# Reordering the first loads and splitting more of the first feed-forward group in a fused recurrence and ReGLU kernel

## Chip, cores and metric

The kernel runs on one core of one Trainium2 chip. The metric is device time in microseconds of one execution: the median of the runs made, and, beside it, one profiled execution whose trace gives the starts and durations of instructions. Engines: PE is TensorE (matmuls), DVE VectorE, ACT ScalarE, POOL GpSimd, SP SyncE (here it only issues DMAs).

## The reference

```python
# q, k, v, f_logit: (4 batches, 8 heads, 768 steps, 48) float32
f = 1 / (1 + exp(-f_logit))
for t in range(768):
    state = f[:, :, t, :, None] * state + k[:, :, t] (outer) v[:, :, t]
    y[:, :, t] = q[:, :, t] @ state
x = y with the heads side by side                    # (3072 tokens, 384)
out = (relu(x @ w_gate) * (x @ w_val)) @ w_out       # d_ff = 1536
```

A gated linear recurrence with a decay for each channel is followed, token by token, by a feed-forward layer with a gate.

## The kernel before

**Units.** The recurrence is cut into chunks of 128 steps. A unit `u` is two chunks of one batch (`y` = 0 and 1); `seq` gives the order of the 12 units: the first unit of each of the four batches (0 to 3), then the second ones, then the third. A unit loads f, k, v and q (`load`, L578, four DMAs of 384 KB on SP), takes exponential and logarithm of f on ACT (L669, L671), sums them along time on PE ("sums", L678, L679; for units with `even` on DVE one half is subtracted on DVE, L682), takes the exponentials of the sums and of their negatives on ACT (L690 to L700), and multiplies k and q by them on DVE or POOL ("products", `hats`, L712, L718). The products are transposed into `qkT`, on PE with a copy by DVE or ACT for the units in `pe_hats` (L770, L780), and by DMA on SP for the others. PE then forms the scores (L806), which are masked either on DVE straight from PSUM (L820) or by a copy on ACT and a product on POOL (L815, L817). Copies of v with padding (`vpad`, and `vrest` for `pe_hats` units, L753, L758) feed the state update (L860 or L871, then L638 to L646) and the output of the unit (`out_of`: 32-column form, L904, for chunks in `pe_x`, else the natural form, L911 and L915, with a DMA transpose). "Totals" (L843, L847) give the decay over a chunk; units with `td` get it through DRAM (`rates`, L827, L836) instead.

**Feed-forward groups.** Two units make a group of 512 tokens. `ffn_hidden` (L940) runs for each of 12 blocks of 128 hidden channels three matmuls for the gate (L952 with `wg`), a relu on ACT (L958), three matmuls for the value (L952 with `wv`) and a product on DVE (L964). A "triple" below is one such set of three matmuls. `ffn_out` (L969) runs the output projection with `wo` (L980, three matmuls a step) and DMAs the result. All feed-forward matmuls are in one chain, so their order is fixed. In the first group, blocks 0 to 2 are run twice on halves of 256 tokens (first unit 0's, then unit 1's), and blocks 3 to 11 on all 512.

**Weights.** Each of `w_gate`, `w_val` and `w_out` is loaded in four slices of three blocks (`wg0` to `wg3` and so on), with conversion to bf16, by DMAs that POOL issues (`load_w`, L606). The string `first` gives the order of the first loads: one order for SP's loads, one for POOL's slices. `x@y` means that the issuing engine waits for the landing of y before it issues x. A load on SP also waits for the landing of the load eight places before it (L577). Engines are in order: everything behind a waiting issue on SP or POOL waits too.

**Order.** The whole program is put in order when it is built: `Plan.schedule` runs a model of the engines, the PSUM banks and the two DMA queues (`Rings`), picks the next instruction by the time it could start and a priority, and writes out a fixed order for each engine. `Plan.limits` gives how many PSUM banks each kind may hold (`f`: feed-forward). Durations in the model (`occ`, `lat`, `RATE`) only decide the order. `EASY` and `slack` add time to modelled DMA landings after a given time. `pace` holds back the sums of a unit until a given block of the feed-forward work. Up to 24 us of modelled time, gaps of PE are filled with matmuls on zeros (L1050, "fillers").

```python
first = 'f0 k0 v0 q0 v1 f1 q3 q1 k1 wg0@k1 wv0@k0 wg1@f0 wv1@k0 wg2@f0 wv2@q0 wg3@q3 wo0@k0 wv3@f0 q2 wo2@q2 wo3@k0 wo1@f1 f2 k2 f3 k3@wg0 v2 v3'.split()
...
behind = list(after) + (sent[-8:][:1] if len(sent) >= 8 else [])
...
for r0, r1, js in {0: [(0, 2, range(0, 3)), (2, 4, range(0, 3)), (0, 4, range(3, 12))]}.get(g, [(0, GC, range(NJ))]):
    for at, j in enumerate(js):
        ffn_hidden(g, r0, r1, j)
```

Of the kernel before, what the change touches and what calls it, by code (L numbers as in the profile page):

```python
# [52 lines left out]
class Rings:  # L53


    CAP, LAND = 3300, 1.0
    RATE = {"hw": (1.0, 0.21), "sw": (1.0, 0.69)}
# [3 lines left out]
    def __init__(self):  # L61
        self.now = 0.0
        self.passed = 0
        self.coming = []
        self.queue = {r: [] for r in self.RATE}
        self.left = {r: 0.0 for r in self.RATE}
        self.out = {r: 0 for r in self.RATE}
        self.n = 0
# [9 lines left out]
    def speed(self, ring):  # L78
        return self.RATE[ring][1 if self.queue[self.OTHER[ring]] else 0]

    def worked(self, t, ring):
        work = t - self.now
        if ring == "sw":
            return work
        for p in self.PAUSES[self.passed:]:
            if p >= t:
                break
            work -= max(0.0, min(t, p + self.PAUSE) - max(self.now, p))
        return work

    def later(self, work, ring):
        t = self.now
        if ring == "sw":
            return t + work
        for p in self.PAUSES[self.passed:]:
            if t + work <= p:
                break
            work -= max(0.0, p - t)
            t = max(t, p + self.PAUSE)
        return t + work  # L100

    def next(self):
        found = None
        for r, q in self.queue.items():
            if q:
                t = self.later(self.left[r] / self.speed(r), r)
                if found is None or t < found[0]:
                    found = (t, r)
        if self.coming and (found is None or self.coming[0][0] < found[0]):
            found = (self.coming[0][0], None)  # L110
        return found

    def step(self, t, ring):
        speeds = {r: self.speed(r) for r in self.RATE}
        for r, q in self.queue.items():
            if q:
                self.left[r] -= self.worked(t, r) * speeds[r]
        self.now = t
        while self.passed < len(self.PAUSES) and self.PAUSES[self.passed] + self.PAUSE <= t:
            self.passed += 1  # L120
        if ring is None:
            _, _, op = self.coming.pop(0)
            q = self.queue[op.ring]
            q.append(op)
            if len(q) == 1:
                self.left[op.ring] = op.flow
            return None
        op = self.queue[ring].pop(0)
        self.out[ring] -= op.descs
        if self.queue[ring]:  # L130
            self.left[ring] = self.queue[ring][0].flow
        return op


class Plan:
# [56 lines left out]
    def schedule(self, banks):  # L192
# [46 lines left out]
        while True:  # L239
# [20 lines left out]
            if event is not None and (pick is None or event[0] <= pick[0][0]):  # L260
                op = rings.step(*event)
                if op is not None:
                    op.end = event[0] + rings.LAND + (op.slack if op.start > self.EASY else 0.0)
                    tell(op, False)
                    for w in waiting["SP"]:
                        if w.flow is not None and w.held:
                            w.ready = max(w.ready, event[0])
                continue
# [101 lines left out]
def bass_hgrn2_outer__then__ffn_reglu_kernel(  # L370
# [14 lines left out]
    HD = H * D  # L385
# [12 lines left out]
    first = 'f0 k0 v0 q0 v1 f1 q3 q1 k1 wg0@k1 wv0@k0 wg1@f0 wv1@k0 wg2@f0 wv2@q0 wg3@q3 wo0@k0 wv3@f0 q2 wo2@q2 wo3@k0 wo1@f1 f2 k2 f3 k3@wg0 v2 v3'.split()  # L398
    seq = [(0, 0), (1, 0), (2, 0), (3, 0), (0, 1), (1, 1), (2, 1), (3, 1), (0, 2), (1, 2), (2, 2), (3, 2)]
    pe_hats = {0, 1, 2, 3, 5}  # L400
    pe_x = {0, 1, 2, 3, 4, 5, 7, 8, 9, 10, 11, 12, 13, 15, 22, 23}
    q_lined = {0, 1, 3, 5, 7, 8, 9, 10}
# [21 lines left out]
    vrow = [sb(f"vrow{i}", [128, 2, HD], BF16) for i in range(2 if any(e.get("vpe") for e in {0: {'kps': False, 'qps': False, 'q0': 'POOL', 'q1': 'POOL', 'even': 'PE', 'm00': 'DVE', 'm01': 'DVE', 'm10': 'DVE', 'tk': 'DVE', 'm11': 'DVE', 'r1': 'POOL', 'tq': 'ACT', 'v11': 'ACT', 'v10': 'DVE', 'r0': 'ACT', 'v01': 'ACT', 'v00': 'DVE1', 'vb': 'DVE1', 'pr': False, 'o1': 'DVE', 'vc0': 'DVE', 'x0': 'ACT', 'x1': 'ACT', 'yy': True, 'o0': 'ACT', 'vc1': 'ACT'}, 1: {'kps': True, 'r0': 'ACT', 'm01': 'DVE', 'm00': 'DVE', 'tq': 'DVE', 'v11': 'POOL', 'even': 'PE', 'tk': 'ACT', 'q1': 'DVE', 'v00': 'DVE1', 'm11': 'POOL', 'r1': 'DVE', 'm10': 'DVE', 'v01': 'POOL', 'v10': 'POOL', 'q0': 'POOL', 'qps': False, 'yy': False, 'td': False, 'vb': 'DVE', 'vc0': 'DVE', 'o0': 'DVE', 'vc1': 'DVE', 'x0': 'ACT', 'o1': 'ACT'}, 2: {'tk': 'DVE', 'v01': 'POOL', 'kps': True, 'r1': 'ACT', 'r0': 'ACT', 'even': 'PE', 'q0': 'DVE', 'v00': 'POOL', 'v10': 'ACT', 'm00': 'DVE', 'v11': 'DVE1', 'm01': 'POOL', 'm11': 'POOL', 'tq': 'DVE', 'q1': 'POOL', 'm10': 'POOL', 'qps': True, 'x0': 'ACT', 'vc1': 'ACT', 'pr': False, 'vc0': 'DVE', 'o0': 'DVE', 'x1': 'ACT', 'vb': 'POOL'}, 4: {'v10': 'DVE1', 'v01': 'POOL', 'm00': 'DVE', 'q11': 'POOL', 'q00': 'POOL', 'q01': 'POOL', 'q0': 'POOL', 'kps': True, 'even': 'DVE', 'm01': 'DVE', 'v00': 'ACT', 'm10': 'POOL', 'q10': 'POOL', 'q1': 'POOL', 'm11': 'POOL', 'v11': 'DVE1', 'qps': False, 'tq': 'DVE', 'r0': 'ACT', 'tk': 'DVE', 'r1': 'ACT', 'yy': True, 'o1': 'ACT', 'o0': 'DVE', 'x1': 'DVE', 'x0': 'DVE'}, 10: {'m00': 'POOL', 'm10': 'POOL', 'q0': 'POOL', 'kps': True, 'q10': 'POOL', 'm01': 'POOL', 'q11': 'POOL', 'q00': 'POOL', 'v11': 'ACT', 'even': 'DVE', 'v01': 'DVE1', 'v00': 'POOL', 'q01': 'POOL', 'q1': 'POOL', 'm11': 'DVE', 'v10': 'ACT', 'td': True, 'o0': 'DVE'}, 9: {'v11': 'ACT', 'v10': 'ACT', 'even': 'DVE', 'kps': True, 'q1': 'POOL', 'm10': 'DVE', 'v00': 'ACT', 'm11': 'POOL', 'q11': 'POOL', 'm00': 'DVE', 'q00': 'POOL', 'q10': 'POOL', 'q0': 'POOL', 'q01': 'POOL', 'v01': 'DVE1', 'm01': 'DVE', 'yy': False, 'x0': 'DVE', 'td': True, 'o0': 'DVE'}, 3: {'kps': True, 'm00': 'DVE', 'm11': 'POOL', 'v11': 'DVE1', 'm10': 'POOL', 'tk': 'ACT', 'v01': 'DVE1', 'r1': 'DVE1', 'tq': 'DVE', 'q1': 'POOL', 'v00': 'DVE1', 'v10': 'POOL', 'q0': 'POOL', 'r0': 'DVE1', 'm01': 'DVE', 'even': 'DVE', 'qps': False, 'vb': 'DVE1', 'x1': 'ACT', 'o1': 'DVE', 'vc1': 'ACT', 'pr': False, 'vc0': 'DVE', 'o0': 'ACT'}, 5: {'q1': 'POOL', 'm00': 'DVE', 'kps': True, 'q11': 'POOL', 'v10': 'ACT', 'v00': 'DVE1', 'even': 'DVE', 'q01': 'POOL', 'm11': 'POOL', 'q00': 'POOL', 'q0': 'POOL', 'v11': 'POOL', 'm01': 'DVE', 'q10': 'POOL', 'v01': 'ACT', 'm10': 'DVE', 'tq': 'ACT', 'r0': 'DVE1', 'tk': 'DVE', 'r1': 'DVE1', 'qps': False, 'o1': 'ACT', 'x0': 'DVE', 'o0': 'ACT', 'yy': False}, 11: {'q0': 'POOL', 'v01': 'ACT', 'q10': 'POOL', 'm00': 'DVE', 'q01': 'POOL', 'm11': 'POOL', 'q1': 'POOL', 'q00': 'POOL', 'kps': True, 'v11': 'ACT', 'm01': 'DVE', 'q11': 'POOL', 'even': 'DVE', 'v00': 'DVE1', 'm10': 'POOL', 'v10': 'DVE1', 'yy': True, 'o1': 'DVE', 'td': True}, 7: {'v10': 'POOL', 'kps': True, 'q1': 'POOL', 'v01': 'POOL', 'q11': 'POOL', 'm00': 'DVE', 'v11': 'DVE1', 'even': 'PE', 'm10': 'POOL', 'm11': 'DVE', 'm01': 'POOL', 'q10': 'POOL', 'qps': False, 'q01': 'POOL', 'q0': 'POOL', 'o0': 'DVE', 'x1': 'DVE', 'td': True, 'x0': 'ACT', 'o1': 'ACT'}, 8: {'m10': 'DVE', 'v11': 'ACT', 'q01': 'POOL', 'm01': 'POOL', 'even': 'DVE', 'q0': 'POOL', 'v10': 'ACT', 'q1': 'POOL', 'm00': 'DVE', 'kps': True, 'q11': 'POOL', 'q00': 'POOL', 'qps': False, 'v00': 'DVE1', 'q10': 'POOL', 'v01': 'ACT', 'pr': False, 'td': True, 'x0': 'DVE'}, 6: {'v10': 'DVE1', 'v01': 'DVE1', 'q10': 'DVE', 'm10': 'DVE', 'kps': True, 'q1': 'DVE', 'even': 'PE', 'q01': 'POOL', 'm00': 'POOL', 'm01': 'POOL', 'q11': 'DVE', 'q00': 'DVE', 'm11': 'POOL', 'qps': True, 'q0': 'DVE', 'pr': False, 'o0': 'DVE', 'yy': False, 'o1': 'DVE'}}.values()) else 0)]  # L424
# [38 lines left out]
    pl = Plan({'bc': 3, 'tp': 1, 's': 4, 'y': 3, 'kv': 4, 'f': 4, 'hot': 1, 'vp': 1})  # L463
    pl.EASY = 30
# [543 lines left out]
    for g in range(NW // GC):  # L1008
        for x in range(GC // 2):
# [3 lines left out]
            for op in pl.ops[before:]:  # L1013
                op.slack = 1.5 if op.flow is not None else 0
# [128 lines left out]
```

## Time and profile before

| | |
|---|---|
| median of 3 runs (range) | 195.18 us (194.57 to 195.86) |
| profiled execution | 193.87 us, span of the instructions 192.1 us |
| granted TensorE clock | 1.0 |
| busy: PE, DVE, ACT, POOL | 183.4, 129.2, 121.6, 82.5 us |
| SP's DMA queue | 28.08 MB, 60.8% of 16 engines' span |
| POOL's DMA queue (weights) | 3.54 MB, 11.8% |

The profile has a page (busy time in 40 slices of the span, DMA rates, the chain of work that ended last, the costliest groups of instructions, DMA issues) and a trace that can be asked for an engine's instructions in a stretch of time. A line of such a timeline gives start, duration, engine, source line, operation, output and inputs, and in brackets idle time ahead of it with what ended it. A line of stretches gives start:end, length, busy time with the number of instructions for PE, PE's weight loads, DVE, ACT and POOL, the granted clock, the busy share of the DMA engines and GB/s. Fillers count as busy.

### The profile page before, as it was taken

What the parts mean: (1) busy time and instruction counts of PE and PEld (TensorE: products, weight loads), DVE (VectorE), ACT (ScalarE), POOL (GpSimd) and SP (SyncE); (2) the same over time, 40 slices, a digit from 0 to 9 for tenths busy, and PEclk for the clock granted to TensorE, in tenths of its full rate; (3) what the DMA queues carried; (4) which work ended last, traced back from release to release, by engine and by line L of the source; (5) the groups of instructions that cost most, each with busy time, mean ns of one, the idle gap of its engine ahead of it and who ended that gap; (6) DMA issues with size and microseconds to landing.
All of it is one profiled execution on the core that took longest, in us unless ns stands there. A gap on an engine that the chain in (4) does not pass through costs nothing.

```text
span 192.1 us, 4498 instructions
## 1 busy us (share of the span) xinstructions
PE 183.4 (95%) x1755; PEld 101.6 (53%) x1777; DVE 129.2 (67%) x238; ACT 121.6 (63%) x233; POOL 82.5 (43%) x110
## 2 busy tenths in 40 slices
PE   7897899999999999999999999999999999999995
PEld 2355584555654546554655556555555455554564
DVE  4579876778798999994689999553485613444311
ACT  4888868785779989948999357456252553333311
POOL 5379867362435257725878695124040600000000
PEclk9999999999999999999999999999999999999999
DMA  5999999999999999998698975422209110111114
GB/s 154 325 325 274 214 205 205 204 230 248 235 311 285 207 320 232 309 239 160 172 258 230 172 154 118 84 77 61 62 5 149 41 44 0 41 43 41 43 42 123
DMA packets 79089, 31.90 MB, mean 166 GB/s; under 512 B 71254, under 2 KB 79068, under 8 KB 79068
## 3 DMA queue, kind: packets, MB, share of 16 engines
q1 hardware_dynamic: 74268, 28.08, 60.8%
q0 software_dynamic: 4800, 3.54, 11.8%
q8 instruction: 14, 0.23, 0.5%
q14 instruction: 7, 0.06, 0.1%
HBM read 25.96 MB, written 4.73 MB: 160 GB/s over the span
## 4 chain that ended last, share of the span: by engine, by line
PE 71%; DMA 12%; DVE 8%; POOL 4%; issue 2%; ACT 1%; SPq 1%; DVEq 0%
PE ps L952 37%; PE ps L980 23%; DMA wo<-in_moe_w_out_dram 10%; PE ps L806 3%; DMA v_in<-in_v_dram 2%; DVE hats L718 2%; PE ps L904 2%; DVE gT L964 1%; DVE hats L712 1%; DVE ptm L820 1%; POOL wo L606 1%; PE ps L770 1%; PE ps L860 1%; POOL hats L712 1%; PE ps L915 1%
## 5 line engine op out<-in xcount | busy, mean ns | idle before, releaser
L964 DVE TENSOR_TENSOR gT<-relu,ps 128x512 bf16<-128x512 bf16 (+1 forms) x75 | 49.5, 664 | 36.1 <-PE ps L952 29.5
L958 ACT ACTIVATE relu<-ps 128x512 bf16<-128x512 f32 (+1 forms) x75 | 43.4, 580 | 28.4 <-PE ps L952 27.8
L952 PE MATMUL ps<-xT,wv 128*128 128x512 bf16 (+1 forms) x223 | 58.8, 370 | 0.9 <-DMA wv<-in_moe_w_val_dram 0.7
L952 PE MATMUL ps<-xT,wg 128*128 128x512 bf16 (+1 forms) x207 | 55.4, 370 | 1.4 <-issue 0.5
L980 PE MATMUL ps<-wo,gT 128*128 128x384 bf16 (+2 forms) x300 | 51.6, 320 | 0.1
L980 PEld LDWEIGHTS ps<-wo,gT 128*128 128x128 bf16 x300 | 28.2, 98 | 19.5 <-DMA wo<-in_moe_w_out_dram 0.3
L817 POOL TENSOR_TENSOR ptm<-ptm,seen 128x512 bf16<-128x512 bf16 x21 | 23.9, 1154 | 20.8 <-ACT ptm L815 20.7
L952 PEld LDWEIGHTS ps<-xT,wv 128*128 128x128 bf16 x225 | 21.0, 98 | 22.2 <-DVE hats L712 0.8
L952 PEld LDWEIGHTS ps<-xT,wg 128*128 128x128 bf16 x225 | 20.9, 98 | 20.5
L646 POOL TENSOR_TENSOR st<-ssum,dec 128x384 bf16<-128x384 f32 x16 | 13.2, 828 | 24.7 <-DMA dec<-rates 12.0
L504 ACT ACTIVATE osb<-ps 128x384 f32<-128x384 f32 x13 | 6.3, 488 | 20.2 <-PE ps L980 20.2
L820 DVE TENSOR_TENSOR ptm<-ps,seen 128x512 bf16<-128x512 f32 x27 | 17.1, 684 | 2.2 <-PE ps L806 2.1
L718 POOL TENSOR_TENSOR hats<-q_in,expo 64x384 bf16<-64x384 f32 x16 | 15.9, 994 | 5.6 <-ACT expo L693 4.6
L718 DVE TENSOR_TENSOR hats<-k_in,ps 64x384 bf16<-64x384 f32 x28 | 15.4, 552 | 1.1 <-ACT ps L700 0.6
L712 POOL TENSOR_TENSOR hats<-q_in,expo 128x384 bf16<-128x384 f32 x11 | 10.9, 1005 | 11.5 <-ACT expo L693 11.5
L815 ACT ACTIVATE ptm<-ps 128x512 bf16<-128x512 f32 x21 | 11.5, 599 | 2.5 <-PE ps L806 2.5
L505 DVE COPY osb<-ps 128x384 f32<-128x384 f32 (+2 forms) x12 | 6.3, 523 | 9.9 <-PE ps L980 9.8
L502 DVE TENSOR_REDUCE vpad<-v_in 64x384 bf16<-64x384 f32 x17 | 9.3, 545 | 4.3 <-DMA v_in<-in_v_dram 3.6
L693 ACT ACTIVATE expo<-ps 128x384 f32<-128x384 f32 x20 | 9.1, 492 | 4.6 <-DVE ps L682 3.9
L669 ACT ACTIVATE f_in<-f_in 128x768 f32<-128x768 f32 x12 | 10.1, 841 | 1.1 <-DMA f_in<-in_f_logit_dram 1.0
L700 ACT ACTIVATE ps<-ps 128x384 f32<-128x384 f32 x22 | 10.3, 491 | 0.0
L671 ACT ACTIVATE bneg<-f_in 128x768 bf16<-128x768 f32 x12 | 10.1, 842 | 0.1
(86 smaller groups left out, 185.9 us busy)
## 6 DMA issues: line engine op xcount, KB each, us to landing
f_in<-in_f_logit_dram SPq DMA_DIRECT2D x12, 384.0 KB, 5.2
k_in<-in_k_dram SPq DMA_DIRECT2D x12, 384.0 KB, 4.9
v_in<-in_v_dram SPq DMA_DIRECT2D x12, 384.0 KB, 5.6
q_in<-in_q_dram SPq DMA_DIRECT2D x12, 384.0 KB, 4.9
out_dram<-osb SPq DMA_DIRECT2D x15, 192.0 KB, 2.4
out_dram<-osb SPq DMA_DIRECT2D x16, 96.0 KB, 2.2
wg<-in_moe_w_gate_dram POOLq DMA_DIRECT2D x4, 288.0 KB, 9.8
wv<-in_moe_w_val_dram POOLq DMA_DIRECT2D x4, 288.0 KB, 9.7
```

Source lines behind the costliest of these rows:

```text
L646: add(e, lambda: engine[e].tensor_tensor(t4(s_new), t4(tmp), rate, ALU.mult), [key] + dk, [f"S{b}_{y}"], prio=P + 2, **(dict(occ=0.79, lat ...
L669: add("ACT", lambda cut=cut: sc.activation(raw["f"][:, cut], raw["f"][:, cut], AF.Exp, scale=-1.0), [f"f{li}"], [f"f{li}"], prio=P, **act_ ...
L700: add("ACT", lambda i=i, ex=ex: sc.activation(bc[i].ap[:, 0:HD] if in_place else ex[:, 1, :], bc[i].ap[:, 0:HD], AF.Exp, scale=1.0), [bc[i ...
L712: add(e, lambda i=i, n=n, x=x, e=e, exps=exps: engine[e].tensor_tensor(hats[:, hi, i, x, :, 0:D], by_i[n][:, i, :, :], exps(), ALU.mult), ...
L718: op = add(e, lambda i=i, n=n, x=x, e=e, y=y, lo=lo, exps=exps: engine[e].tensor_tensor(hats[64 * i:64 * i + 64, hi, y, x, :, 0:D], by_i[n ...
L815: add("ACT", lambda pt=pt, s=sj[j]: sc.activation(pt, s.ap[:, :].rearrange("p (n t) -> p n t", n=NP), AF.Copy), [sj[j]], [f"raw{mis[y]}_{j ...
L817: add("POOL", lambda pt=pt, mask=mask: gp.tensor_tensor(pt, pt, mask, ALU.mult), [f"raw{mis[y]}_{j}", "seen"], [f"raw{mis[y]}_{j}", f"ptm{ ...
L820: add("DVE", lambda pt=pt, mask=mask, s=sj[j]: ve.tensor_tensor(pt, s.ap[:, :].rearrange("p (n t) -> p n t", n=NP), mask, ALU.mult), [sj[j ...
L952: mm = te.matmul(bank.ap[:, 0:n], wt[:, kt, j * 128:(j + 1) * 128], xT[xi][:, kt, n0:n1], start=(kt == 0), stop=(kt == NK - 1))
L958: add("ACT", lambda: sc.activation(relu[ri][:, 0:n], gate.ap[:, 0:n], AF.Relu), [gate], [f"relu{ri}"], prio=P, **act_t(n))
L964: add("DVE", lambda: ve.tensor_tensor(gT[gi][:, j, n0:n1], relu[ri][:, 0:n], val.ap[:, 0:n], ALU.mult), [val, f"relu{ri}"], [f"gT{gi}_{j}_ ...
L980: mm = te.matmul(bank.ap[:, 0:cut[1] - cut[0]], gT[gi][:, j, r * C:(r + 1) * C], wo[:, j, cut[0]:cut[1]], start=(j == 0), stop=(j == NJ - 1))
```

## The change

The model of the DMA queues gets other numbers and a slower state of POOL's queue when it starts; the loads get another order with other waits; eight of the first group's twelve blocks are run by halves; PSUM limits, priorities, pacing and the engine for many copies, products and masks are chosen anew. What is computed is the same. Lines of the changed kernel stand five lower than those of before (L952 becomes L957).

```diff
-    CAP, LAND = 3300, 1.0
-    RATE = {"hw": (1.0, 0.21), "sw": (1.0, 0.69)}
+    CAP, LAND, SPREAD, INSIDE = 3300, 1.0, 0.45, 0.3
+    RATE = {"hw": (1.0, 0.208), "sw": (1.0, 0.668)}
+    COLD = {"hw": (1.0, 0.36), "sw": (0.83, 0.53)}
...
-    first = 'f0 k0 v0 q0 v1 f1 q3 q1 k1 wg0@k1 wv0@k0 wg1@f0 wv1@k0 wg2@f0 wv2@q0 wg3@q3 wo0@k0 wv3@f0 q2 wo2@q2 wo3@k0 wo1@f1 f2 k2 f3 k3@wg0 v2 v3'.split()
+    first = 'f0 k0 v0 q0 wv0@q0 wg0@q0 wg1@f0 wg2@k0 wv2@k0 f1 q1 k1 wv1@k1 wg3@f0 v1 f2@wv2 v2 wo1@v2 k2 wo0@k2 wv3@f0 f3@wv1 q2@wv2 wo3@q2 wo2@k2 k3@wg2 q3@wo1 v3'.split()
...
-    pe_x = {0, 1, 2, 3, 4, 5, 7, 8, 9, 10, 11, 12, 13, 15, 22, 23}
-    q_lined = {0, 1, 3, 5, 7, 8, 9, 10}
+    pe_x = {0, 1, 2, 3, 4, 6, 7, 8, 9, 11, 15, 18, 19, 22, 23}
+    q_lined = {0, 1, 2, 3, 6, 7, 8, 10}
...
-    pl = Plan({'bc': 3, 'tp': 1, 's': 4, 'y': 3, 'kv': 4, 'f': 4, 'hot': 1, 'vp': 1})
-    pl.EASY = 30
+    pl = Plan({'bc': 3, 'tp': 2, 's': 4, 'y': 2, 'kv': 4, 'f': 5, 'hot': 1, 'vp': 1})
+    pl.EASY = 60
...
-        behind = list(after) + (sent[-8:][:1] if len(sent) >= 8 else [])
+        behind = list(after) + (sent[-4:][:1] if len(sent) >= 4 else [])
...
-        op = chain("load_w", "POOL", ..., occ=0.79, lat=2.3,
+        op = chain("load_w", "POOL", ..., occ=0.79, lat=1.85,
...
-        dma(op, f"{nm}{s}", 0.483 * size, ring="sw")
+        dma(op, f"{nm}{s}", 0.492 * size, ring="sw")
...
     (the three feed-forward chains)
-              prio=P + 60, opens=[gate])
+              prio=P + 20, opens=[gate])
...
-                op.slack = 1.5 if op.flow is not None else 0
-        for r0, r1, js in {0: [(0, 2, range(0, 3)), (2, 4, range(0, 3)), (0, 4, range(3, 12))]}.get(g, [(0, GC, range(NJ))]):
+                op.slack = 3 if op.flow is not None else 0
+        for r0, r1, js in {0: [(0, 2, range(0, 8)), (2, 4, range(0, 8)), (0, 4, range(8, 12))]}.get(g, [(0, GC, range(NJ))]):
...
-    pace = {6: 21, 10: 24, 5: 3, 8: 31, 9: 23, 11: 49}
+    pace = {9: 18, 5: 15, 11: 45, 7: 21, 3: 3, 4: 9}
```

A table with a line for each unit, repeated in the code, says which engine does what. Of its many changes these are spoken of below (key: before, after):

```
unit 0:  q0, q1 (query products): POOL, DVE     kps, qps (exponentials in PSUM): False, True
         m01 (mask of y=0, second half): DVE, POOL
         vpe (v spread by PE from one whole copy, with the matrices ident and swap): none, True   vb (engine of that copy): POOL
unit 7:  td: True, none       unit 10: td: True, none (qps: none, True)
```

The changed order, as built, on the two issuing engines (`x <- y`: x is issued after y has landed):

```
SP:   f0 k0 v0 q0, f1 <- f0, q1 <- k0, k1 <- v0, v1 <- q0, f2 <- f1 wv2, v2 <- q1, k2 <- k1, f3 <- v1 wv1,
      q2 <- f2, k3 <- wg2 v2, q3 <- k2 wo1, v3 <- f3, f4 <- q2, ...
POOL: copy of v0, wv0 <- q0, wg0, wg1, wg2, wv2, wv1 <- k1, state product, wg3, mask, copy of v1, mask, state product,
      wo1 <- v2, copy of v2, wo0 <- k2, wv3, two copies of v2, wo3 <- q2, wo2, products of q2, ...
PE:   ... output of unit 0 (both chunks), transposes of unit 1, 5 triples, scores, 1, 1, scores, state, output y=0 of unit 1,
      4 triples, output y=1, 10 triples, sums and total of unit 2, 9 triples, transposes of k2, state of unit 2, 2 triples,
      gate of block 8, sums and total of unit 3, value of block 8, transposes of q2, gate and value of block 9, scores of unit 2, ...
```

## The prediction

> **What bounds the kernel now.** I read the page's rows of busy tenths first, then the chain that ended last, the PE timeline around the start of the feed-forward work, and the stretches of the DMA side.
>
> ```profile
> PE   7897899999999999999999999999999999999995
> ...
> GB/s 154 325 325 274 214 205 205 204 230 248 235 311 285 207 320 232 309 239 160 172 258 230 172 154 118 84 77 61 62 5 149 41 44 0 41 43 41 43 42 123
> ```
>
> One digit is 4.8 us. From the sixth on PE is full, so past about 29 us the time is the sum of PE's work. What is left to win lies in the first 29 us, where a part of "busy" is filler matmuls on zeros (L1050). The PE timeline shows where useful work becomes dense:
>
> ```profile
> 21.31 0.41 PE L904 MATMUL ps<-ptm,vpad 128*32 128x128 bf16 x16 [0.24 <-DVE ptm L820]
> 21.65 0.50 PE L952 MATMUL ps<-xT,wg 128*128 128x256 bf16 x3
> 22.08 0.35 PE L904 MATMUL ps<-qkT,st 128*32 128x128 bf16 x12
> 22.26 0.40 PE L904 MATMUL ps<-ptm,vpad 128*32 128x128 bf16 x16
> 23.32 0.49 PE L952 MATMUL ps<-xT,wv 128*128 128x256 bf16 x3 [0.66 <-DMA wv<-in_moe_w_val_dram]
> ...
> 53.88 0.59 PE L952 MATMUL ps<-xT,wg 128*128 128x512 bf16 x2
> ```
>
> The first feed-forward matmul runs at 21.65, the second waits for a weight slice until 23.32, and the second group begins at 53.88. The DMA side is full all that time:
>
> ```profile
> 9.00:10.00 1.00, 1.00 (x11) 0.43 (x8) 0.91 (x2) 0.99 (x3) 1.00 (x2) 1.00 1.17 323
> 22.00:23.00 1.00, 0.66 (x30) 0.40 (x28) 0.89 (x3) 1.00 (x4) 1.00 (x2) 1.00 1.32 204
> 30.00:31.00 1.00, 1.00 (x6) 0.47 (x5) 0.56 (x1) 1.00 (x3) 1.00 (x2) 1.00 1.27 208
> ```
>
> The last column is GB/s: 323 with SyncE's loads alone, 204 in a stretch in which nearly only weight slices moved (270 packets of GpSimd's queue against 11 of SyncE's), 208 with both (184 against 180). A load of 384 KB alone takes 1.21 us at 325 GB/s. A slice of 288 KB took 2.2 us beside loads (landings at 27.4, 29.6, 31.8, 34.0, 36.1, 38.4: issue time plus time to landing of each) and 1.5 us in the unmixed stretch (288 KB at some 200 GB/s). Beside slices a load took 5.8 us (landings 25.2, 31.9, 37.6).
>
> ```profile
> 14.22 0.93 POOL L606 DMA_DIRECT2D wg<-in_moe_w_gate_dram  x1 [1.08 <-DMA k_in<-in_k_dram]
> ...
> 26.60 18.27 DMA wo<-in_moe_w_out_dram
> ```
>
> The first slice is issued at 14.22 and lands 6.7 us later; the last is issued at 26.60 and lands at 44.9, and the chain that ended last runs through it.
>
> **The change, step by step.** I walk the changed order with the rows of before.
>
> (1) *First weights.* Unit 0's four loads land as before (4.2, 5.4, 6.6, 7.9). GpSimd now waits for q0, not for k1, so its first slice (wv0) is issued at 7.9 instead of 14.2. GpSimd first copies v0 whole: 128x768, no row; its 64x384 cast is 0.50, twice that is 1.0, hidden before 7.9. Unit 1's loads wait each for a landing of unit 0, four in flight, landing at 9.1, 10.3, about 12 and, slowed by the first slice, 15. With 6.7 us for the first slice, wv0 lands at 14.6, wg0 at 16.4 (between 1.5 and 2.2), then alone at 1.5: wg1 17.9, wg2 19.4, wv2 20.9, wv1 22.5. Bounds for wv1: 21.5 (all at 1.5) and 25.6 (all at 2.2). f2 is queued behind wv2's landing, and with it all of SyncE's later loads.
>
> (2) *Unit 0.* Four added PE matmuls (v0 spread by ident and swap, 0.16 each) stand in place of a filler, and ACT and DVE lose four copies of 0.36 to 0.55. Against that, the first unit's query products move from GpSimd to DVE (4 x 0.51 in a row, from 7.5 to 9.5) and GpSimd's mask of y=0 stands behind seven DMA issues (0.78 each) and a state product: it ends at 15.5. The masks of y=1 on DVE end at 15.7. Unit 0's output matmuls start at 15.75 where they started at 15.31: 0.45 later. Unit 1's transposes follow (to 17.65), and the first feed-forward matmul starts at 17.65, when wg0 (16.4) has landed: 4.0 earlier than now.
>
> (3) *Halves.* Eight blocks by halves instead of three give 60 more matmuls of 256 columns (0.109) for 30 fewer of 512 (0.2157): +0.07. In exchange 16 blocks' pairs (32 x 0.327) can run on unit 0's and then unit 1's tokens alone. Five triples run to 19.3; then PE waits on ACT, whose queue holds two 1.02 transposed copies and a copy of v ahead of the first relu (0.9 lost); scores, state and y=0 of unit 1 run to 22.05; the fourth block's val matmul waits for wv1, which is the last of the six: 22.5, 0.45 lost. Then 3 triples, y=1 of unit 1 (0.5) and 10 triples end at 27.6. By then the useful work, counted from start to start in the timeline, is 14.0 us: units 0 and 1 at 3.57 each (sums 0.65, totals 0.2, transposes 0.88, scores 0.55, state 0.45, output 0.84) and 21 triples at 0.327. The old order had 12.6 by 27.6: the two units, 14 triples and 0.87 of unit 2. The lead is 1.4.
>
> (4) *Units 2 and 3 come later.* f2 is issued at 20.9, its data start at 22.2 beside the seventh slice (wg3, to 24.1), it lands at 25.2 instead of 16.8; v2 26.4, k2 27.6, f3 28.8, q2 30. ACT's exponentials of f2 (0.84 each) sit between relus, so a late f2 would stop the relus and PE with them; at 25.2 the cumulative sum of unit 2 runs at 27.6, unhindered. In the next 6 us ACT has 2 x 1.7 for f2 and f3, four 0.49 and nine 0.38: 8.8 us. PE has other work for most of it, I take 0.3 lost (bounds 0 and 2.8).
>
> (5) *The six last slices.* wo1 waits on GpSimd for v2 (26.4), and behind it stand wo0, wv3, wo3, wo2, two copies of v2, unit 2's query products and masks. Issued at 26.5, wo1 lands at 33.2 by the 6.7 of the first slice (nothing moves on that queue since 24.1, so it starts anew), wo0 at 35.4, wv3 at 37.6. I take 37.1, as part of the 6.7 was a fuller ring of loads; bounds 34.5 (three slices at 1.5 after 31.5) and 38.6. PE reaches the val matmul of block 9, which needs wv3, at 35.9: from 27.6, 9 triples (2.95), sums and totals of two units (1.4), two transposes and a state (1.35), one half pair and one whole (1.95) and gate 9 (0.65). So 1.2 is lost, give or take 1.2.
>
> The Trainium skill (DMA: Bandwidth & Descriptors, section on the anatomy of a SWDGE DMA) prices a GpSimd-issued DMA at a fixed 2.0 us plus bytes over 436 GB/s. For the 576 KB read that gives an estimate of 3.4 us from issue to landing; this trace has 6.7 for the first slice. By the page wv3 would come 3.3 us sooner, step 5 would cost nothing, and the sum would be 1.2 lower.
>
> (6) *To the second group.* From 37.1: the rest of group 0's hidden blocks, unit 2's output, and 48 output triples' worth of matmuls (7.8 us) with unit 3 between. q3 waits for wo1 and then shares the queue: it lands at 42, its products end at 44, unit 3's scores run at 47.1, its output at 50.9 to 51.4. The second group begins at 52.8 against 53.88: 1.1 earlier.
>
> (7) *Later.* PE gets two more totals (units 7 and 10 no longer fetch rates by DMA; 0.2 each), and one output more in the natural form (-0.33 -0.34 +0.34 +0.2 = -0.13): with step 3's 0.07 that is +0.34. Engine choices for masks and copies move between DVE, ACT and GpSimd at equal work; PE covers them (DVE 88 of 128 us, ACT 80, GpSimd 49 after 53.88). Without that cover they'd cost; between 60 and 80 us DVE was busy 9.61 of 10, so bounds 0 and 2. The end (60 output matmuls, copy, store) is unchanged.
>
> Sum: -1.1 + 0.34 = -0.75 us. The profiled execution took 193.87 (span 192.1 and 1.8 around it); the median of the runs shown is 195.18, 1.3 above. On the median's scale: 194.4.
>
> **Rivals.**
> - *The waits close (faster).* No loss at wv1, ACT or wv3. For it: the unmixed 1.5 us slice is a row. Against: the 6.7 of a first slice is one too. Gain 1.1 + 1.2 + 0.45 + 0.3 - 0.34 = 2.7: 192.5.
> - *The second half of the weights comes late (slower).* Place: wo1 behind v2 on GpSimd. For it: a load beside slices took 11 us (f3: issued 13.93, landed 25.2). If v2 lands at 29.5 rather than 26.4, wv3 lands at 40.2 and PE stands 3.1 longer: 193.13 + 3.1 = 196.2 profiled, 197.5. It decides against the change once v2 is later than 27.2. Against: only one slice is left moving when v2 starts.
> - *The hold does nothing.* The bytes are the same, and a held slice plus the load's share (0.38 of 1.21) is 1.5 + 0.46 = 2.0 against 2.2. If unit 2 and 3 then only move the wait, the lead of 1.4 is given back by 53.88: 193.87 + 0.34, or 195.5.
>
> **Chances and range.** Runs of this kernel spread over 0.7%, so 1% (2 us) is about what can be told from no change. Forecast and the hold that does nothing, both within 1%: 0.42. Waits close: 0.33, faster by over 1%. Weights late, or DVE in the way after 60 us: 0.25, slower by over 1%. The likeliest case alone spans 193.3 to 196.3; the range of 8 in 10 reaches into both others, 191.8 to 197.2.
>
> **What would show it.** Right: the first matmul of L957 near 17.7, a wait of PE for wv near 22 and again near 36 to 37, wo1 landing near 33, the second group at 52 to 53.5, filler count 28 instead of 33. Wrong: v2 landing after 28, PE idle of over 2 us between 28 and 45, or PE idle after 54 us of more than 1 us over now (1.4 of 127.9).

## The result and the profile after

| | before | changed |
|---|---|---|
| median of 20 runs each, side by side | 194.39 us | 195.61 us |
| ratio changed to before (95% interval) | | 1.0047 (1.0025 to 1.0068) |
| profiled execution, span of its instructions | 193.87, 192.1 us | 195.38, 193.7 us |
| first feed-forward matmul | 21.65 us | 17.62 us |
| start of the second group | 53.88 us | 54.50 us |
| start of the last output matmul | 189.53 us | 191.06 us |

The changed kernel is slower by half a per cent: 0.0047 x 194.4 = 0.9 us by the ratio, 1.5 us between the two profiled executions. The medians are of all twenty runs, while the ratio leaves out four runs of the changed kernel whose granted clock was lowered (0.983 to 0.991). The forecast was 0.75 us shorter. Feed-forward work begins 4.0 us sooner, as forecast, and by the second group all of that has gone.

In the page of the changed kernel, the rows of PE and of GB/s by slices of 4.84 us:

```profile
PE   7889899699999999999999999999999999999995
...
GB/s 155 324 257 203 214 266 228 238 233 223 334 294 221 304 286 103 297 300 240 256 234 166 195 109 64 43 83 88 51 115 68 44 41 0 41 42 44 41 41 122
```

The new thing is the 6 in the eighth slice (34 to 39 us), where the row of before was full. GB/s falls to 203 in the fourth slice, where before still had 274: the weights now go ahead of units 2 and 3. PE's timeline shows the three places that the prediction named:

```profile
17.62 0.49 PE L957 MATMUL ps<-xT,wg 128*128 128x256 bf16 x3
...
22.72 0.49 PE L957 MATMUL ps<-xT,wv 128*128 128x256 bf16 x3 [0.64 <-DMA wv<-in_moe_w_val_dram]
...
34.80 0.81 PE L957 MATMUL ps<-xT,wv 128*128 128x512 bf16 x3
37.14 0.62 PE L775 MATMUL ps<-ident,hats 128*128 128x128 bf16 x8 [1.54 <-POOL hats L717]
37.60 0.81 PE L957 MATMUL ps<-xT,wg 128*128 128x512 bf16 x3
38.25 0.81 PE L957 MATMUL ps<-xT,wv 128*128 128x512 bf16 x3
...
54.50 0.81 PE L957 MATMUL ps<-xT,wg 128*128 128x512 bf16 x3
```

The first matmul and the wait for wv1 are where they were put (17.65 and 22.5). The wait near 36 is there, but not for a weight: the eight transposes of q2 wait for q2's products on POOL (L717). The chain that ended last leads from there back to q2:

```profile
25.35 7.89 DMA q_in<-in_q_dram
...
33.53 0.43 POOL wo L611
...
34.30 0.77 POOL wo L611
...
35.14 1.95 POOL hats L717 x2
...
37.14 0.62 PE ps L775 x8
```

q2 took 7.9 us from issue to landing. POOL was not free to use it at once: the issue of wo3 had itself waited for q2, so two issues (0.78 each) went ahead of the products. What moved beside q2 can be read from POOL's timeline:

```profile
26.81 0.80 POOL L611 DMA_DIRECT2D wo<-in_moe_w_out_dram  x1 [2.53 <-DMA v_in<-in_v_dram]
...
29.05 0.78 POOL L611 DMA_DIRECT2D wo<-in_moe_w_out_dram  x1 [0.89 <-DMA k_in<-in_k_dram]
29.82 0.77 POOL L611 DMA_DIRECT2D wv<-in_moe_w_val_dram  x1
...
33.53 1.55 POOL L611 DMA_DIRECT2D wo<-in_moe_w_out_dram  x2 [1.81 <-DMA q_in<-in_q_dram]
```

v2 landed at 26.5 and k2 at 28.8; each landing let slices go (wo1, then wo0 and wv3), and these shared the DMA engines with q2. That they are what made q2 slow is not shown. In the traces of experiments 4 and 5 and of the repeat of experiment 2 three slices are issued at nearly the same times, and q2 took 5.1 to 5.4 us; in both traces of the changed kernel it took 7.6 to 7.9. No run moves q2 without slices beside it.

**Where the time went.** I add up PE's useful instructions in their order, each at the usual start-to-start time of its kind; what a start lies behind that sum is time that PE idled, turned from one kind to another, or ran fillers. The trace of before lacks some 20 matmul records (1755 matmuls, 1777 weight loads); these count as work.

| up to | work, before / changed | idle and filler, before / changed |
|---|---|---|
| 27.9 us | 12.6 / 14.4 | 15.27 / 13.48 |
| start of the second group | 37.77 / 38.27 | 16.11 / 16.23 |
| start of the last output matmul | 172.52 / 173.27 | 17.01 / 17.79 |

At 27.9 us the changed kernel has idled 1.79 us less; 0.43 of this went into spreading v0 by PE (four matmuls, two at a time, from 7.67 to the next start at 8.11), so its lead is 1.36. From there to the second group it idles 2.75 against 0.84: 1.69 at q2's transposes, the other 1.06 in gaps of about 0.1 where PE turns from one kind of matmul to another. After the second group it has 0.26 more work and 0.66 more idle time.

### The profile page after: what moved, and what is told of

The parts are those of the page before. It is cut to its first block, busy times and chain, and to the rows that moved or that the text cites. A ratio compares the mean times of both kernels' runs of the same rounds, so it can differ in the third digit from the quotient of the medians.

```text
span 193.7 us, 4564 instructions
## 1 busy us (share of the span) xinstructions
PE 186.0 (96%) x1800; PEld 104.6 (54%) x1800; DVE 130.0 (67%) x246; ACT 120.5 (62%) x236; POOL 80.8 (42%) x113
## 4 chain that ended last, share of the span: by engine, by line
PE 77%; DMA 14%; POOL 3%; ACT 2%; SPq 1%; issue 1%; DVE 1%
PE ps L957 41%; PE ps L985 25%; DMA q_in<-in_q_dram 7%; DMA wv<-in_moe_w_val_dram 5%; PE ps L811 3%; PE ps L909 3%; DMA f_in<-in_f_logit_dram 2%; PE ps L775 1%; POOL wg L611 1%; SPq L583 1%; PE ps L865 1%; POOL hats L717 1%; PE ps L920 1%; ACT ptm L820 1%; PE ps L916 1%
## 5 line engine op out<-in xcount | busy, mean ns | idle before, releaser
L957 PE MATMUL ps<-xT,wv 128*128 128x512 bf16 (+1 forms) x240 | 59.8, 358 | 0.6 <-DMA wv<-in_moe_w_val_dram 0.6
L957 PE MATMUL ps<-xT,wg 128*128 128x512 bf16 (+1 forms) x240 | 59.8, 358 | 0.1
L822 POOL TENSOR_TENSOR ptm<-ptm,seen 128x512 bf16<-128x512 bf16 x24 | 27.3, 1155 | 27.8 <-ACT ptm L820 27.8
L957 PEld LDWEIGHTS ps<-xT,wv 128*128 128x128 bf16 x240 | 22.3, 98 | 21.3 <-DVE st L643 0.8
L957 PEld LDWEIGHTS ps<-xT,wg 128*128 128x128 bf16 x240 | 22.4, 98 | 19.5 <-ACT ptm L820 0.5
L509 ACT ACTIVATE osb<-ps 128x384 f32<-128x384 f32 (+2 forms) x16 | 7.5, 469 | 20.4 <-PE ps L985 20.4
L825 DVE TENSOR_TENSOR ptm<-ps,seen 128x512 bf16<-128x512 f32 x24 | 15.5, 684 | 6.0 <-PE ps L811 5.9
L820 ACT ACTIVATE ptm<-ps 128x512 bf16<-128x512 f32 x24 | 13.1, 598 | 3.6 <-PE ps L811 3.5
L717 POOL TENSOR_TENSOR hats<-q_in,expo 128x384 bf16<-128x384 f32 x10 | 9.8, 998 | 6.6 <-ACT expo L698 6.5
L510 POOL CAST vpad<-v_in 64x384 bf16<-64x384 f32 x19 | 9.5, 500 | 2.2 <-PE ps L920 1.2
L648 DVE TENSOR_TENSOR ssum<-ps,st 128x384 f32<-128x384 f32 x16 | 8.8, 550 | 0.1
L1055 PE MATMUL ps<-zeros 128*128 128x512 bf16 x28 | 8.4, 450 | 0.4 <-DVE hats L717 0.4
## 6 DMA issues: line engine op xcount, KB each, us to landing
out_dram<-osb SPq DMA_DIRECT2D x14, 192.0 KB, 3.2
```

The costliest lines, as they stand in the source:

```text
L717: add(e, lambda i=i, n=n, x=x, e=e, exps=exps: engine[e].tensor_tensor(hats[:, hi, i, x, :, 0:D], by_i[n][:, i, :, :], exps(), ALU.mult), ...
L820: add("ACT", lambda pt=pt, s=sj[j]: sc.activation(pt, s.ap[:, :].rearrange("p (n t) -> p n t", n=NP), AF.Copy), [sj[j]], [f"raw{mis[y]}_{j ...
L822: add("POOL", lambda pt=pt, mask=mask: gp.tensor_tensor(pt, pt, mask, ALU.mult), [f"raw{mis[y]}_{j}", "seen"], [f"raw{mis[y]}_{j}", f"ptm{ ...
L825: add("DVE", lambda pt=pt, mask=mask, s=sj[j]: ve.tensor_tensor(pt, s.ap[:, :].rearrange("p (n t) -> p n t", n=NP), mask, ALU.mult), [sj[j ...
L957: mm = te.matmul(bank.ap[:, 0:n], wt[:, kt, j * 128:(j + 1) * 128], xT[xi][:, kt, n0:n1], start=(kt == 0), stop=(kt == NK - 1))
```

## Experiments

Unless said otherwise, these keep the built order of every engine and change only what is shown, right after the order is made: `no_wait(x, y)` lets x be issued without waiting for y, `wait_for` adds such a wait, `swap_places` exchanges two instructions of an engine. Every ratio is to the kernel before, run beside it. The executions of one kernel spread over some 2 us, so a trace tells of one of them; for the main readings I took a second one. Gains of a few tenths of a microsecond are read from traces: the ratios of most of these runs have intervals that overlap.

**1. wo3 no longer waits for q2.**

```diff
+    no_wait("wo3", "q2")
```

> The changed kernel with every engine's order kept; only GpSimd's wait for the landing of q2 ahead of the slice wo3 is dropped, so that wo3 and wo2 are issued at about 31.7 instead of 33.5. Theory (the lead is lost where unit 2's query products stand on GpSimd behind two weight issues that wait for q2): the products start at q2's landing, 33.5 instead of 35.1, the transposes of q2 on PE at 35.6 instead of 37.1, and then PE waits for wv3 (landed at 37.7) at the value of block 9, about 0.9 us: 0.5 us faster than the changed kernel. Rival 1 (q2's late landing is the cause, not what stands behind it): more slice traffic makes q2 later, no gain or 0.5 slower. Rival 2 (PE's added matmuls cost the time, waits of PE are covered): no difference over 0.2 us.

Measured: 195.03 us, ratio 1.0036 (1.0012 to 1.0059); span 192.8, second group at 53.62, 0.88 sooner than in the changed kernel (by the ratios alone the two can't be told apart). PE's timeline:

```profile
34.85 0.81 PE L957 MATMUL ps<-xT,wv 128*128 128x512 bf16 x3
35.49 0.61 PE L775 MATMUL ps<-ident,hats 128*128 128x128 bf16 x8
35.94 0.81 PE L957 MATMUL ps<-xT,wg 128*128 128x512 bf16 x3
37.36 0.82 PE L957 MATMUL ps<-xT,wv 128*128 128x512 bf16 x3 [0.61 <-DMA wv<-in_moe_w_val_dram]
```

The wait for POOL is gone and the next one appears: the val matmul of block 9 for wv3, the wait of the prediction's step 5, with 0.8 from start to start (35.94 + 0.65 to 37.36) instead of 1.2. So two waits stood close behind each other, and POOL's came last.

**2. The same, and wv3 issued ahead of wo1.**

```diff
+    no_wait("wo3", "q2")
+    swap_places("POOL", done["wo1"], done["wv3"])
+    no_wait("wo1", "v2");  wait_for("wv3", "v2")
+    no_wait("q3", "wo1");  wait_for("q3", "wv3")
```

> As the run without the wait for q2, and wv3 and wo1 change places in GpSimd's queue (wv3 first, wo1 third; q3 waits for wv3 instead of wo1, so that it is issued at the same time). Theory: both waits of PE between 35 and 38 us go, wv3 lands near 33, wo1 near 37.7 where it is needed at 44: 1.5 us faster than the changed kernel, 0.3 to 0.7 faster than the kernel before. Rival 1 (bytes decide, not order): PE waits for another slice or for q3 before 50 us instead, gain under 0.5. Rival 2 (added matmuls): under 0.2.

Measured: 194.23 us, ratio 1.0018 (0.9994 to 1.0041), span 192.0. Run again later beside experiment 9:

> The two edits alone (wo3 no longer behind q2, wv3 issued ahead of wo1), repeated beside the run with the totals by transfer. Both theories: second feed-forward group at 52.8 us again, span 192.0, ratio to the kernel before 1.000 to 1.003.

194.70 us, ratio 1.0046 (1.0022 to 1.0071), span 192.1, second group at 53.19. The first of the two traces:

```profile
35.44 0.61 PE L775 MATMUL ps<-ident,hats 128*128 128x128 bf16 x8
35.88 0.81 PE L957 MATMUL ps<-xT,wg 128*128 128x512 bf16 x3
36.53 0.81 PE L957 MATMUL ps<-xT,wv 128*128 128x512 bf16 x3
...
52.81 0.81 PE L957 MATMUL ps<-xT,wg 128*128 128x512 bf16 x3
```

With both waits gone the second group starts at 52.81, where the forecast had put it. Still the kernel is not faster than before: its last output matmul starts at 189.38 (before: 189.53), as 0.90 us less idle time meets 0.75 us more work. The timed runs say the same, or a little worse: medians 0.3 and 0.8 above those of before, against 1.2 for the changed kernel. Both traces are of executions near the lowest of their runs (193.70 and 193.86), so what the others wait for isn't seen. Five runs have these exchanges in the built order (this one, its repeat, and, with more exchanged, experiments 5 and 6 and the repeat of 6); their medians lie 0.3 to 0.8 above before. Those of the changed kernel, its repeat and experiments 1 and 4 lie 1.1 to 1.3 above. By the timed runs the two waits together are thus worth some 0.6 us, about half of the loss, where the traces have 1.2 to 1.7 at the last output matmul. The lowest single times are 193.54 and 193.81, before 193.40, the changed kernel 194.36.

**3. SyncE's loads no longer held back for weight slices (q3 alone still waits for wo1).**

```diff
+    no_wait("f2", "wv2");  no_wait("f3", "wv1")
+    no_wait("q2", "wv2");  no_wait("k3", "wg2")
```

> The changed kernel with SyncE's queue not held: f2, f3, q2 and k3 no longer wait for weight slices, only for the load four places before (q3 still waits for wo1); every engine's order kept. Theory: f2, v2, k2 flow beside the six slices, a slice takes 2.2 instead of 1.5, wv1 lands 2 to 3 us later (24.5 to 25.5) and PE's wait at 22.7 grows by that much, while the wait at 37 goes since q2, v2 and wo1 are 3 or more us earlier: the end within 1 us of the changed kernel, either sign. Rival (holding the queue is itself what costs): 1.5 us or more faster than the changed kernel, and faster than the kernel before.

Measured: 199.38 us, ratio 1.0266 (1.0238 to 1.0294); second group at 58.50. Neither theory had it so large. PE's timeline, then stretches (columns as before: the granted clock is the third number from the right):

```profile
26.22 0.80 PE L957 MATMUL ps<-xT,wv 128*128 128x256 bf16 x3 [4.21 <-DMA wv<-in_moe_w_val_dram]
```

```profile
23.00:24.00 1.00, 0.00 (x0) 0.00 (x0) 0.62 (x2) 0.00 (x0) 0.63 (x1) 1.00 1.24 203
24.00:25.00 1.00, 0.00 (x0) 0.00 (x0) 0.00 (x0) 0.00 (x0) 0.20 (x1) 0.61 1.24 204
...
30.00:31.00 1.00, 1.00 (x7) 0.69 (x6) 0.85 (x2) 0.00 (x0) 0.97 (x2) 0.50 1.29 240
31.00:32.00 1.00, 1.00 (x10) 0.91 (x9) 0.38 (x3) 0.77 (x2) 0.92 (x2) 0.97 1.26 235
```

Unit 2's loads share the DMA engines with the first slices, and wv1, the last of the six, comes 3.5 us later. In that wait the granted clock falls to half, and stays there until 31: from 26.2 to 31.05 PE works at half speed, some 2.4 us lost. So the hold does what it says; of its 4.0 us at the second group up to 2.4 are the clock's. The rival "the hold does nothing" is out, although its time (195.5) is the one nearest to the measured median.

**4. wv1 fourth instead of sixth.**

```diff
+    no_wait("wv1", "k1")
+    swap_places("POOL", done["wg2"], done["wv1"])
```

> The changed kernel with the slices wv1 and wg2 in each other's place in GpSimd's queue (wv1 fourth, wg2 sixth; wv1 no longer waits for k1); all else kept. Theory: PE's wait of 0.64 at 22.7 for wv1 goes, but PE then only arrives earlier at the wait for the transposes of q2 at 37.1, which does not move: end within 0.2 us of the changed kernel. Rival (PE is work-bound from the first feed-forward matmul on, so each wait counts): 0.6 us faster.

Measured: 195.24 us, ratio 1.0053 (1.0035 to 1.0072), second group at 54.21. The wait at 22.7 is gone, and PE reaches the sums of unit 2 earlier than they can start:

```profile
27.83 0.34 PE L683 MATMUL ps<-bneg,upto 128*128 128x384 bf16 x1 [0.55 <-ACT bneg L676]
...
36.05 0.61 PE L775 MATMUL ps<-ident,hats 128*128 128x128 bf16 x8
...
37.95 0.82 PE L957 MATMUL ps<-xT,wv 128*128 128x512 bf16 x3 [0.65 <-DMA wv<-in_moe_w_val_dram]
```

The 0.64 us only move: with units 0 and 1 exhausted, f2 is what PE comes to next, and f2 did not become earlier. The theory had PE arrive earlier at the wait for q2's transposes, and that is not what came. q2 landed at 31.3 instead of 33.2, although the order and the waits behind the first slices are those of the changed kernel; its transposes ran unhindered at 36.05, and PE waited for wv3 instead, the wait of the prediction's step 5. So q2's stall is not fixed by the order, and where it is missing the next waits take up most of its time: the second group starts only 0.3 sooner.

**5. Both, 2 and 4.**

> The two edits together on the changed kernel: no wait for q2 ahead of wo3 with wv3 first of the last slices, and wv1 fourth, wg2 sixth. Theory: with the wait at 37 us gone, the 0.64 at 22.7 is no longer covered; but the run with wv1 fourth alone showed that unit 2's sums then wait 0.55 for f2 at 27.8. So 0.1 to 0.3 us faster than wv3 first alone. Rival (all waits of PE add up): 0.6 faster than wv3 first alone.

Measured: 194.42 us, ratio 1.0009 (0.9984 to 1.0033); second group at 53.36, last output matmul at 189.71. No gain over experiment 2 can be seen; the expected 0.1 to 0.3 is missing from the trace too, which is 0.3 longer.

**6. f2 released by the fourth slice instead of the fifth, on top of 5.**

```diff
+    no_wait("f2", "wv2");  wait_for("f2", "wv1")
```

> As both edits together, and f2 waits for wv1, now the fourth slice, instead of wv2, the fifth: SyncE's queue is held for four slices. Theory: f2 and all behind it come 1.4 us earlier, unit 2's sums no longer wait at 27.8, v2 and with it the last six slices come earlier; the fifth and sixth slice cost 2.2 each instead of 1.5 and land at 22 and 24.5, when PE needs them at 24 to 24.5: 0.3 to 0.7 us faster than both edits with the hold of five slices, 0.5 to 1 faster than the kernel before. Rival (a shorter hold is a step to no hold, which cost 4 us): PE waits for wg2 or wv2 by 0.5 or more, slower than both edits.

Measured: 194.45 us, ratio 1.0018 (0.9989 to 1.0046). The profiled execution was the longest of its twelve (196.01), so I ran it again:

> The kernel in which f2 waits for the fourth slice, again, for a second trace; its first trace was of the slowest of its 12 executions (196.01 us; the median was 194.45). Theory (q3 is late there as a rule): again a wait of over 1 us at the transposes of unit 3's q products near 46 us, the second group after 54.5. Rival (that wait belonged to one execution): no wait over 0.7 us, the second group at 52.5 to 53.5, span 192 to 192.5, a ratio to the kernel before of 0.999 to 1.003.

194.63 us, ratio 1.0035 (1.0011 to 1.0058), second group at 53.28. The transposes of q3 in the first trace and in the second:

```profile
46.45 0.62 PE L775 MATMUL ps<-ident,hats 128*128 128x128 bf16 x8 [1.41 <-POOL hats L717]
```

```profile
44.62 0.62 PE L775 MATMUL ps<-ident,hats 128*128 128x128 bf16 x8 [0.27 <-POOL hats L717]
```

So q3's lateness belonged to one of the two executions, and the hoped-for gain is missing in both: f2 is issued over 1 us sooner than in the changed kernel (19.97 and 19.73 against 21.16), and no time comes off.

**7. Three blocks by halves instead of eight, with the new loads; planned anew.**

```diff
-    {0: [(0, 2, range(0, 8)), (2, 4, range(0, 8)), (0, 4, range(8, 12))]}
+    {0: [(0, 2, range(0, 3)), (2, 4, range(0, 3)), (0, 4, range(3, 12))]}
```

> The changed kernel with three blocks of the first group by halves instead of eight; the order is made anew by the same planner. Theory: only 6 triples instead of 11 can run before unit 1's output is there, PE idles some 1.6 us more before 25 us, and 60 matmuls of 256 columns fall away (0.07): 1 to 1.7 us slower than the changed kernel, unless the later wait at 37 covers it, then 0 to 0.5. Rival (halves cost more than they give): faster than the changed kernel.

Measured: 196.39 us, ratio 1.0109 (1.0065 to 1.0153), second group at 56.95. PE runs out of unit 0's triples and turns to fillers:

```profile
21.67 1.25 PE L1055 MATMUL ps<-zeros 128*128 128x512 bf16 x5
24.21 0.50 PE L957 MATMUL ps<-xT,wg 128*128 128x256 bf16 x3 [0.73 <-DVE xT L510]
```

So giving up the halves costs some 1.2 us with these loads (ratios 1.0109 and 1.0047, whose intervals just touch), and 2.5 us at the second group in the traces, of which this one is of the longest of its six executions (197.52). How much of it belongs to the halves and how much to the new order I can't tell.

**8. Eight blocks by halves in the kernel before; planned anew.**

> The kernel before with eight blocks by halves instead of three; loads as before; order made anew by its planner. Theory: its first feed-forward matmul comes at 21.65, when unit 1's output is 1 us away, and its slices arrive every 2.2 us while a block of two halves takes 1.3: the halves give nothing: within 0.3 us of the kernel before, if the order made anew is as good. Rival (halves are the gain and the loads the loss): 0.5 us or more faster.

Measured: 197.57 us, ratio 1.0162 (1.0114 to 1.0209); expected was no difference. The first feed-forward matmul starts at 22.34 and PE waits for operands in seven places before 33 us, of which two:

```profile
18.14 0.61 PE L770 MATMUL ps<-ident,hats 128*128 128x128 bf16 x8 [0.94 <-POOL hats L712]
...
27.93 0.62 PE L806 MATMUL ps<-qkT 48*128 48x128 bf16 x16 [0.79 <-DVE qkT L505]
```

The first of these comes before any halved block can run, so the new order itself is worse; this run doesn't price the halves. (Its trace, too, is of the longest of six executions, 198.46.)

**9. Experiment 2 with the totals of unit 7 by transfer again; planned anew.**

```diff
+    (table of units)  unit 7: 'td': True     unit 10: 'td': True
```

> The changed kernel with the two edits of the run before (wo3 no longer behind q2, wv3 issued ahead of wo1) and with the totals of units 7 and 10 taken by a transfer again, as in the kernel before; planned anew, with the order unchanged up to unit 6's sums. Theory (what is left of the loss is work that TensorE was given): the two groups of totals on TensorE cost 0.20 us each, so 0.4 us shorter than the run with the two edits alone, last output matmul 0.4 earlier, a profiled span near 191.6 and a ratio to the kernel before of 0.998 to 1.000. Rival (TensorE has room there, since it idles 0.66 us more after 54 us in waits for masks and copies): within 0.1 us of the run with the two edits.

The edit sets both units, but only unit 7 changed: the code takes the transfer only where `qps` is not set, and unit 10 has it set. The trace has eight groups of totals on PE, the changed kernel nine, the kernel before seven.

Measured: 195.28 us, ratio 1.0080 (1.0047 to 1.0113): 0.6 above the repeat of experiment 2 in the median, though the intervals overlap; neither theory had it slower. Up to the second group (52.88) nothing moved; after it PE idles 2.9 us instead of 1.6, and the largest piece is

```profile
109.80 0.34 PE L865 MATMUL ps<-vpad,hats 128*128 128x96 bf16 x4 [0.79 <-DVE hats L723]
```

The new plan asked for a state update before its operand was there. This doesn't show the totals to be free or dear; it shows that the order after 54 us can cost more than the 0.2 us of one group of totals.

**10. The changed kernel again.**

> The changed kernel itself again, for a second trace: its executions spread over 2 us. Theory (a fixed lateness of q2 behind wo1, wo0 and wv3): the transposes of unit 2's q products come at 37 us after a wait of 1.2 to 2 us on the chain q2, wo3's issue on GpSimd, the products, and the second group starts at 54 to 55 us. Rival (that wait belonged to one execution): another wait, or none over 0.7 us, between 34 and 40 us, and a second group near 53.

Measured: 195.04 us, ratio 1.0056 (1.0035 to 1.0077), span 193.3. The waits come again, with the second one a little shorter:

```profile
22.67 0.49 PE L957 MATMUL ps<-xT,wv 128*128 128x256 bf16 x3 [0.73 <-DMA wv<-in_moe_w_val_dram]
...
36.83 0.62 PE L775 MATMUL ps<-ident,hats 128*128 128x128 bf16 x8 [1.28 <-POOL hats L717]
...
54.18 0.81 PE L957 MATMUL ps<-xT,wg 128*128 128x512 bf16 x3
```

## Why the prediction missed

- *Step 1, first weights: right.* wv0 was issued at 8.27 (put at 7.9) and PE got wv1 at 22.7 (put at 22.5). Two prices in it were off and made up for each other: the first slice took 5.5 us instead of 6.7, and the five behind it came 1.8 us apart (13.7 to 22.7) instead of 1.6. The Trainium skill (DMA: Bandwidth & Descriptors, section on the anatomy of a SWDGE DMA) gave the prediction an estimate of 3.4 us for it; neither trace agrees, as the fastest of their slices took 5.5.
- *Steps 2 and 3: right.* First triple at 17.62 (17.65), wait for wv1 0.64 (0.45), sums of unit 2 at 27.92 (27.6), lead 1.36 (1.4). The four matmuls that spread v0 took 0.43 us; putting them in place of a filler, at no cost, was right, since PE idles around them.
- *Step 4: failed at q2.* f2 (put at 25.2, its sums unhindered) and v2 (26.4, landed at 26.5) were right. k2 was put at 27.6 and came at 28.8; q2 was put at 30 and came at 33.2, and at 32.9 in the second trace. The step gave each load 1.2 us of an unshared queue up to 30, although step 5 let wo1 go at 26.5. The row of 5.8 us for a load beside slices was in the text, and was not used here. (Its landings, 25.2, 31.9 and 37.6, lie 6.7 and 5.7 apart.) The sharing need not be all of it: with as many slices beside it q2 landed at 30.8 to 31.3 in experiments 4 and 5 and the repeat of 2, and what makes the other 2 us stays open.
- *Step 5: slices right, wait wrong.* wo1 to wv3 came as put: the data of wv3 ended at 37.3, the matmul that needs it ran at 38.25 unhindered in the changed kernel and at 37.36 in experiment 1 (put: 37.1). But q2's transposes, listed in the order ahead of block 9, were taken as ready. "wo3 <- q2" stands in the order of POOL with "products of q2" two issues behind it; these two were never added to q2's path (33.53 + 1.55 + 1.95 = 37.03). It took both errors: PE was ready for the transposes at 35.45, and with q2 at 30 the two issues would have been hidden, as would q2 at 33.2 without them (33.53 + 1.95 = 35.48). The loss there was 1.69 instead of 1.2.
- *Step 6: failed with 4 and 5.* 52.8 was forecast; 54.50 and 54.18 came. 52.81 and 53.19 came where both waits were taken away. That is less of a confirmation than it looks: the forecast held 1.5 us of losses (0.3 at ACT, 1.2 at wv3) which experiment 2 doesn't have. In their place stand some 1.1 us of gaps of about 0.1 at PE's turns between kinds of matmul, counted as nothing, and the 0.3 by which the sums of unit 2 came later. So the forecast of the start was 1.7 too early, which is about the length of q2's stall, and its other losses were of the right sum and the wrong kind: luck. Nor does that stall alone decide: in experiment 4, without it, the second group still starts at 54.21.
- *Step 7: too small.* Of the 0.34 that was put, 0.07 is the halves' and lies before the second group; against the 0.27 behind it 0.92 came: 0.26 of work and 0.66 more idle time. The bounds (0 and 2) held it. Taking each matmul's time up to the next start, the two added groups of totals with the turns behind them are 0.58 of the 0.92 (0.40 was put), and the output in natural form saves 0.06 (0.13 was put). The other 0.4 is spread over turns between kinds, and its cause was not found: PE's waits there are so short that the list of waits after 54 us is empty for the changed kernel. The idle time is the same in experiment 2 (1.56 after the second group in both, 0.90 before), so it isn't a consequence of the late q2.

Sum: a lead of 1.36, less 1.91 in waits and gaps beyond those of before and 0.07 of work: the second group 0.62 later; then 0.92 more: 1.54 at the last output matmul. The scale added to the miss: the forecast stood on a median of 195.18 from three runs, and twenty gave 194.39. That 195.61 lies within the stated range, and even within the likeliest case's own span (193.3 to 196.3), is owed to their width; the direction was wrong.

Of the rivals, "the second half of the weights comes late" named the right stretch and the wrong piece: v2 landed at 26.5, before its point of decision (27.2). The time of "the hold does nothing" was met for another reason: experiment 3 shows the hold to be worth much.

## What to carry to other kernels

When loads are moved behind one another, price each with what its own landing releases: v2's landing let slices go, and q2 beside them landed 0.8 to 3.2 us later than put, by the execution. Follow the last operand of a unit through every issue that stands ahead of its use on the same engine; an issue that waits for x, placed ahead of the instruction that uses x, puts its own time into x's path. And a time saved before the bounding engine is full is worth only what no later wait takes back, less any work added to that engine: here, even with both waits taken away, 0.90 us less idle time met 0.75 us more work.

## What the runs showed of the hardware

- *The granted clock in a long wait.* In experiment 3 PE had no matmul from 22.0 to 26.2 us. The clock went from 1.0 to 0.5 at 24.22, 2.2 us after the last matmul, and back at 31.05, 6.8 us later, though PE was busy again from 26.2. The Trainium skill (TensorE: Matmul & The Clock Gate, part 1) says that the clock is set by activity in free-running windows of 3.4 us, half after an idle window and full after a busy one. The 6.8 us agree with two such windows, the first of them with PE busy for 1.42 of 3.42 us and the second full; the window that would have ended at 24.22 was not empty, though, with PE busy for 1.00 of 3.41 us. Waits of 1.5 us (changed kernel) left the clock at 1.0.
- *Loads beside slices.* In the changed kernel q2 took 7.9 us from issue to landing beside three slices, in experiment 5 5.3 us; slices came 1.5 us apart alone (data ended at 15.47, 16.97, 18.45, 19.91, 21.37) and 2.2 to 2.9 mixed (32.47, 35.12, 37.32, 40.26).
